# Linear attention and two MoE layers: low halves on VectorE, and the keys' maxima as a bias

## The chip, the cores and the metric

The kernel runs on one core of a Trainium2 chip. The metric is the device time of one execution in microseconds. Three executions of the kernel before and one profiled execution are at hand. The engines are called TensorE (PE in the rows, PEld for its weight loads), VectorE (DVE), ScalarE (ACT), GpSimd (POOL) and SyncE (SP), which issues most DMAs.

## What is computed

Linear attention over 8 batches, 8 heads, 576 tokens and 64 dimensions comes first, then a dense gated layer, then a layer with 8 experts of which each token takes one. The attention's features are two exponentials of a projection, from which the token's largest absolute value is taken away:

```python
def phi(x):
    proj = np.einsum('bhsd,df->bhsf', x, w_phi)
    proj = proj - np.max(np.abs(proj), axis=-1, keepdims=True)
    return np.concatenate([np.exp(proj), np.exp(-proj)], axis=-1)
q_p, k_p = phi(q), phi(k)
kv = np.einsum('bhsf,bhsd->bhfd', k_p, v)
z = np.sum(k_p, axis=2)
num = np.einsum('bhsf,bhfd->bhsd', q_p, kv)
den = np.einsum('bhsf,bhf->bhs', q_p, z)[..., None] + 1e-06
x = num / den                      # to tokens x 512
h = ((x @ w1) * (x @ w2)) @ w3
x = h @ w_out
# then: argmax of x @ w_gate, softmax weight, relu(x @ w1[e]) @ w2[e]
```

## The kernel before, in words

Every product on TensorE is made in float16 with operands cut into a high half and a low half: the high half is the value rounded to float16, the low half what is left of it, and three matmuls (high by high, high by low, low by high) make one product. So each operand that is computed on the chip needs one instruction for its high half and one subtraction for its low half.

**Attention** is done for two batches at a time (four units) and, in a unit, two heads at a time (`group`, 16 calls). A group has three steps of three token tiles (`c`) for each head `h`, 96 of them in all. For the keys: `proj` (line 543) multiplies into a PSUM tile `pj`, `k_max` (563) takes the absolute maximum `mk` of each token on VectorE, `k_sub` (569) takes it away from `pj` into an SBUF tile `pm`, `k_exp` (575) makes on ScalarE the exponential of minus `pm` (`ke2`) and, through `exp16`, the exponential of `pm` twice, once rounded to float16 into the tile `k1` and once in float32 into `e1`; `exp_lo` (559) takes one from the other on GpSimd into the low half of `k1`. `k_c1` and `k_c2` scale `ke2` into the two halves of `k2`, and `k_b` multiplies both with the values into `kv`. For the queries: `proj` and `q_max` find the maxima, `q_pj` projects again, transposed, into `pjT`, `q_exp` makes the four activations of two signs with the bias `nM`, `exp_lo` their two low halves `q1` and `q2`, `q_nm` multiplies them with the cut sums `kvs` into `nm`, `q_add` (lines 711 and 712) adds the parts into `nx`, and `q_x` (lines 719 to 723) divides into `xn`.

**The first MoE layer** (`moe1`, 12 calls of three token tiles): `ab` multiplies into two PSUM tiles `pab`, `a_out` copies one of them on ScalarE (`asb`), `g_mul` (817) multiplies on VectorE into `gf`, `g_hi` (821) rounds on ScalarE into `gt`, `g_lo` (824) makes the low half on GpSimd, and `y` (843) multiplies `gt` with the joined weights.

Beside these run the setting up of the weights (`conv64`, `moe_weight`, `w34_setup`) and the cutting of the experts' weights (`expert_weight`: line 321 on ScalarE, line 325 on VectorE, written out to DRAM). When all tokens are routed, `phase_b` runs the experts' slots.

**What sets the order.** Each step is put in a list with a time in units of its own (`at`, table `O`) and the list is written out by those times; the tile framework's scheduler then sets the order of the instructions on each engine. Every engine takes its instructions strictly in its order. Tiles share buffers by tag: `pj`, `pjT` and the experts' sums have three PSUM buffers with the tag `pj`; `nm`, `pv`, `pk`, `pq`, `pe`, `pr` and `pn` share a single one with the tag `ts`; `e1` has three buffers for keys and queries together, `q1` and `q2` two each.

Of the kernel before, what the change touches and what calls it, by code (L numbers as in the profile page):

```python
# [8 lines left out]
F32 = mybir.dt.float32  # L9
F16 = mybir.dt.float16  # L10
# [3 lines left out]
AF = mybir.ActivationFunctionType  # L14
ALU = mybir.AluOpType
# [4 lines left out]
P = 128  # L20
# [31 lines left out]
ES = 1.0 / (QS * WS)  # L52
# [12 lines left out]
def kernel(  # L65
# [16 lines left out]
    V, A, G, T = nc.vector, nc.scalar, nc.gpsimd, nc.tensor  # L82
# [23 lines left out]
    const = ctx.enter_context(tc.tile_pool(name="const", bufs=1))  # L106
    psum = ctx.enter_context(tc.tile_pool(name="psum", bufs=1, space=PSUM))
    stat = ctx.enter_context(tc.tile_pool(name="stat", bufs=2))
# [16 lines left out]
    W_B = const.tile([P, FD], F16, name="W_B")  # L125
    it8 = const.tile([P, NE], F32, name="it8")
    tri8 = const.tile([P, NE, NE], F32, name="tri8")

    def setup_a():
        nc.sync.dma_start(wphi_f[0:64, :], w_phi)  # L130
        nc.sync.dma_start(wphi_f[64:128, :], w_phi)
        V.tensor_scalar(W_A, wphi_f, WS, None, op0=ALU.mult)
        V.scalar_tensor_tensor(W_B, wphi_f, WS, W_A, op0=ALU.mult, op1=ALU.subtract)
        V.memset(zero, 0.0)

    def setup_b():
        make_identity(nc, ident32)
        V.memset(ones16, 1.0)
        V.memset(onesb, 1.0)
        V.memset(ones32, 1.0)  # L140

    def setup_c():
        G.affine_select(
            out=utri, in_=ones16, pattern=[[1, P]], compare_op=ALU.is_gt,
            fill=0.0, base=0, channel_multiplier=-1,
        )
        G.iota(rev8, pattern=[[0, 3], [-1, NE]], base=NE, channel_multiplier=0,
               allow_small_or_imprecise_dtypes=True)
        for b in range(B):
            c0 = 9 * (b // 2) + 5 * (b % 2)  # L150
            p0 = 64 * (b % 2)
            G.iota(ids[:, c0:c0 + 4], pattern=[[1, 4]], base=b * S, channel_multiplier=4)
            G.iota(ids[p0:p0 + 64, 9 * (b // 2) + 4:9 * (b // 2) + 5], pattern=[[0, 1]], base=b * S + 512,
                   channel_multiplier=1)
        G.iota(cumE, pattern=[[RG, NE]], base=0, channel_multiplier=0,
               allow_small_or_imprecise_dtypes=True)
        G.iota(it8, pattern=[[1, NE]], base=0, channel_multiplier=0, allow_small_or_imprecise_dtypes=True)
        V.memset(tri8, 1.0)
        G.affine_select(out=tri8, in_=tri8, pattern=[[1, NE], [-1, NE]], compare_op=ALU.is_ge,
                        fill=0.0, base=0, channel_multiplier=0)  # L160
# [308 lines left out]
    def group(ui, g, T0):  # L469

        bs = units[ui]
        att = pools["att"]
        h0 = 2 * g
        st = {}
# [76 lines left out]
        def exp16(key, src, sgn, nm, bufs, bias=0.0):  # L551

            hl = att.tile([P, 2, 3, P], F16, tag=nm, bufs=bufs, name=nm)
            A.activation(hl[:, 0], src, AF.Exp, scale=sgn * ES, bias=bias)  # L554
            e1 = att.tile([P, 3, P], F32, tag="e1", bufs=3, name="e1")
            A.activation(e1, src, AF.Exp, scale=sgn * ES, bias=bias)  # L556
            st[key] = (hl, e1)

        def exp_lo(key):
            hl, e1 = st[key]  # L560
            G.tensor_tensor(hl[:, 1], e1, hl[:, 0], op=ALU.subtract)  # L561

        def k_max(h, c):
            if c == 0:
# [2 lines left out]
                            apply_absolute_value=True)  # L567

        def k_sub(h, c):
            pm = att.tile([P, 3, P], F32, tag="pm", bufs=2, name="pm")  # L570
            mk = st["mk", h][:, 3 * c:3 * c + 3]
            V.tensor_tensor(pm, st["pj", "kf", h, c], mk.unsqueeze(2).to_broadcast([P, 3, P]), op=ALU.subtract)
            st["pm", h, c] = pm

        def k_exp(h, c):
            pm = st["pm", h, c]
            e2 = att.tile([P, 3, P], F32, tag="ke2", bufs=3, name="ke2")
            A.activation(e2, pm, AF.Exp, scale=-ES)
            exp16(("k1", h, c), pm, 1.0, "k1", 3)
            st["ke2", h, c] = e2  # L580

        def k_s1(h):
# [87 lines left out]

        def q_exp(c, h):
            for z in range(2):
                exp16(("q", c, h, z), st["pjT"], 1.0 - 2.0 * z, "q%d" % (z + 1), 2, st["nM"][:, 3 * h + c:3 * h + c + 1])

        def q_e1():

# [50 lines left out]
        for h in range(2):  # L727
            tv = T0 + 3 * h
            for fn in (v_load, v_norm, v_sum, v_scale, v_hi, v_lo, k_s1, k_s2, k_s3, kv_hi, kv_lo):
                at(tv + O[fn.__name__], fn, h)  # L730
            for c in range(3):
                tk = T0 + 3 * h + c
                at(tk + O["k_proj"], proj, "kf", h, c)
                for fn in (k_max, k_sub, k_exp, k_c1, k_c2, k_b):
                    at(tk + O[fn.__name__], fn, h, c)
                at(tk + O["k_lo"], exp_lo, ("k1", h, c))
        for c in range(3):
            tq = T0 + c
            at(tq + O["k_split"], split, "kf", c)
            at(tq + O["k_trans"], trans, "kf", c)  # L740
            at(T0 + O["q_sc"] * c + O["q_split"], split, "qf", c)
            at(T0 + O["q_sc"] * c + O["q_trans"], trans, "qf", c)
            for h in range(2):
                at(T0 + O["q_proj"] + O["q_pc"] * c + O["q_proj_h"] * h, proj, "qf", h, c)
                at(T0 + O["q_max"] + O["q_pc"] * c + O["q_proj_h"] * h, q_max, c, h)
                th = tq + O["q_h"] * h
                for z in range(2):
                    at(th + O["q_lo"] + O["q_lo_z"] * z, exp_lo, ("q", c, h, z))
                for fn in (q_pj, q_exp, q_nm, q_add):
                    at(th + O[fn.__name__], fn, c, h)  # L750
            at(tq + O["q_x"], q_x, c)
# [41 lines left out]
    def moe1(p, c, tk, s):  # L793
# [3 lines left out]
        st = {}  # L797
        gT = []
# [22 lines left out]
            A.copy(gT[m][:, 0, :], st["gf", m])  # L821

        def g_lo(m):
            G.tensor_tensor(gT[m][:, 1, :], st["gf", m], gT[m][:, 0, :], op=ALU.subtract)  # L824

        cw = 256 if last else 260

# [118 lines left out]
        for m in range(8):  # L946
            t = tk + m * s
            at(t, ab, m, 0)
            at(t + 0.5 * s, ab, m, 1)
            for fn in (a_out, g_mul, g_hi, g_lo):  # L950
                at(t + O[fn.__name__], fn, m)
        for n in range(3):
            t = tk + (8 + n) * s + O["y"]
# [36 lines left out]
    at(t_su * O["su_end"], su_close)  # L990
    at(0, setup_a)
    at(0.1, setup_b)
    at(1, setup_c)
    at(2, setup_d)
# [235 lines left out]
```

## Time and profile before

| | us |
|---|---|
| three executions | 1669.16, 1670.81, 1676.45 (median 1670.81) |
| the profiled execution | 1671.89 |
| its span, first to last instruction | 1670.1 |
| busy in the span: TensorE | 1429.4 (86%) |
| VectorE | 971.0 (58%) |
| ScalarE | 885.9 (53%) |
| GpSimd | 587.5 (35%) |

The shares are means over parts that differ. Attention and the first MoE layer overlap until about 1050 us; the last part of that layer and the last expert weights follow until about 1210 us; from there on the experts' slots run, with TensorE nearly always busy. The span's chain of waits breaks off in the last microseconds at the output's DMAs and tells nothing of the first part. The times of a timeline row are start and duration; an engine's next instruction often starts before the one ahead has ended, so that the distance of two starts is what an instruction takes of the engine.

### The profile page before, as it was taken

How to read it: one execution, taken by the hardware profiler on the slowest of the kernel's cores; microseconds unless marked ns; L12 is line 12 of the kernel's file. 1: busy time of each engine (PE TensorE's matmuls, PEld its weight loads, DVE VectorE, ACT ScalarE, POOL GpSimd, SP SyncE). 2: the span in 40 equal slices, each digit the busy share in tenths (PEclk: the TensorE clock that was granted, in tenths of full speed). 3: DMA queues.
4: the chain of work that ended last, by engine and by line, in shares of the span. 5: the costliest groups of instructions: out<-in, count | busy, mean ns of one | idle time of the engine just before them, and what ended most of it. 6: DMA issues, size and time to landing. Idle time of an engine off the chain costs nothing. (4 is left out here: it accounts for less than half of the span.)

```text
span 1670.1 us, 38442 instructions
## 1 busy us (share of the span) xinstructions
PE 1429.4 (86%) x14854; PEld 1029.5 (62%) x14854; DVE 971.0 (58%) x2647; ACT 885.9 (53%) x1979; POOL 587.5 (35%) x875
## 2 busy tenths in 40 slices
PE   5888868889897688977787989978949999999998
PEld 4655545656565465756465757646647777777776
DVE  6999989968878687777786886532421111111111
ACT  4787798766776567767576777433311111111111
POOL 3546553444543425434344354211312111121110
PEclk9998978989999799989988999979979999999999
DMA  6756255554257653493955464974347345646361
GB/s 198 217 143 170 64 142 124 144 150 146 71 152 124 127 157 92 119 157 89 161 157 89 139 121 112 140 248 102 70 145 188 83 77 174 221 130 173 76 172 31
DMA packets 273044, 225.17 MB, mean 135 GB/s; under 512 B 187221, under 2 KB 244825, under 8 KB 271706
## 3 DMA queue, kind: packets, MB, share of 16 engines
q1 hardware_dynamic: 265306, 202.71, 50.8%
q0 software_dynamic: 7552, 19.97, 4.1%
q8 instruction: 118, 1.93, 0.5%
q14 instruction: 68, 0.56, 0.1%
HBM read 261.22 MB, written 53.67 MB: 189 GB/s over the span
## 5 line engine op out<-in xcount | busy, mean ns | idle before, releaser
L806 PE MATMUL pab<-xT,w 128*128 128x384 f16 x768 | 263.5, 343 | 8.7 <-DVE gf L817 5.6
L1132 DVE SCALAR_TENSOR_TENSOR hT<-ph,hT 128x512 f16<-128x512 f32 x80 | 55.3, 691 | 362.0 <-ACT hT L1131 362.0
L807 PE MATMUL pab<-xT,w 128*128 128x384 f16 x768 | 262.8, 342 | 0.0
L808 PE MATMUL pab<-xT,w 128*128 128x384 f16 x768 | 262.6, 342 | 0.0
L1127 PE MATMUL ph<-xTb,wb 128*128 128x128 f16 x1280 | 218.1, 220 | 22.5 <-DMA xTb<-rw 22.5
L1128 PE MATMUL ph<-xTb,wb 128*128 128x128 f16 x1280 | 218.1, 220 | 0.0
L1129 PE MATMUL ph<-xTb,wb 128*128 128x128 f16 x1280 | 218.1, 220 | 0.0
L843 PE MATMUL py<-w,gt 128*128 128x260 f16 (+1 forms) x1728 | 205.5, 275 | 12.4 <-ACT yb L850 9.2
L561 POOL TENSOR_TENSOR q<-e,q 128x384 f16<-128x384 f32 x192 | 188.7, 992 | 65.1 <-ACT e L556 60.8
L843 PEld LDWEIGHTS <-gt 128*128 128x128 f16 x1728 | 166.3, 99 | 36.4 <-issue 9.3
L824 POOL TENSOR_TENSOR gt<-gf,gt 128x384 f16<-128x384 f32 x96 | 96.2, 1003 | 182.0 <-ACT gt L821 176.6
L561 POOL TENSOR_TENSOR k<-e,k 128x384 f16<-128x384 f32 x96 | 96.4, 1004 | 159.3 <-ACT k L554 89.3
L702 PE MATMUL nm<-kvs,q 128*128 128x65 f16 (+1 forms) x1920 | 90.1, 204 | 70.2 <-DVE nx L712 35.9
L1131 ACT ACTIVATE hT<-ph 128x512 f16<-128x512 f32 x80 | 47.8, 597 | 187.1 <-PE ph L1129 187.1
L1127 PEld LDWEIGHTS <-wb 128*128 128x128 f16 x1280 | 125.8, 98 | 27.7 <-DMA xTb<-rw 21.2
L702 PEld LDWEIGHTS <-q 128*128 128x128 f16 (+1 forms) x1920 | 79.0, 107 | 100.1 <-issue 47.3
L325 DVE SCALAR_TENSOR_TENSOR pc<-wf,ess,pc 128x512 f16<-128x512 f32 x128 | 104.6, 834 | 47.2 <-ACT pc L321 47.0
L1128 PEld LDWEIGHTS <-wb 128*128 128x128 f16 x1280 | 125.8, 98 | 4.5
L554 ACT ACTIVATE q<-pjT,nM 128x384 f16<-128x384 f32 x192 | 114.4, 596 | 26.0 <-PE nm L702 19.6
L1129 PEld LDWEIGHTS <-wb 128*128 128x128 f16 x1280 | 125.8, 98 | 0.0
L1150 ACT ACTIVATE ob<-pob,scb 128x512 f32<-128x512 f32 x40 | 27.5, 688 | 183.4 <-PE pob L1148 183.4
L626 PE MATMUL kv<-vs,k 128*128 128x65 f16 x1920 | 90.6, 198 | 37.5 <-ACT k L604 23.3
(255 smaller groups left out, 3483.6 us busy)
## 6 DMA issues: line engine op xcount, KB each, us to landing
wb<-wscr SPq DMA_DIRECT2D x40, 4096.0 KB
wf<-in_moe_w_dram SPq DMA_DIRECT2D x16, 2048.0 KB
wscr<-pc SPq DMA_DIRECT2D x128, 256.0 KB
raw<-in_moe_w_dram SPq DMA_DIRECT2D x32, 512.0 KB
rows_d<-row SPq DMA_DIRECT2D x32, 256.5 KB
kf<-in_k_dram SPq DMA_DIRECT2D x64, 128.0 KB
vf<-in_v_dram SPq DMA_DIRECT2D x64, 128.0 KB
qf<-in_q_dram SPq DMA_DIRECT2D x64, 128.0 KB
```

The costliest lines, as they stand in the source:

```text
L325: V.scalar_tensor_tensor(pc[:, 1, :], st["wf"][:, j * 512:(j + 1) * 512], st["s"][:, 0:1], pc[:, 0, :], op0=ALU.mult, op1=ALU.subtract)
L554: A.activation(hl[:, 0], src, AF.Exp, scale=sgn * ES, bias=bias)
L561: G.tensor_tensor(hl[:, 1], e1, hl[:, 0], op=ALU.subtract)
L702: T.matmul(nm[p0:p1, t, z, :], lhsT=hl[:, a, t, p0:p1], rhs=st["kvs"][:, b, h, z, bb, :], start=(a == b), stop=bool(a), skip_group_check=True)
L806: T.matmul(ps, lhsT=wh, rhs=xT[:, 0, kk], start=(kk == 0), stop=False)
L807: T.matmul(ps, lhsT=wh, rhs=xT[:, 1, kk], start=False, stop=False)
L808: T.matmul(ps, lhsT=wl, rhs=xT[:, 0, kk], start=False, stop=(kk == 3))
L824: G.tensor_tensor(gT[m][:, 1, :], st["gf", m], gT[m][:, 0, :], op=ALU.subtract)
L843: T.matmul(py, lhsT=gT[i][:, a, t * P:(t + 1) * P], rhs=w34[:, i, b, hf, 0:cw], start=(i == 0 and a == b), stop=bool(i == 7 and a))
L1127: T.matmul(ph[:, mm, :], lhsT=wh, rhs=xT[:, 0, kk, :], start=(kk == 0), stop=False)
L1128: T.matmul(ph[:, mm, :], lhsT=wh, rhs=xT[:, 1, kk, :], start=False, stop=False)
L1129: T.matmul(ph[:, mm, :], lhsT=wl, rhs=xT[:, 0, kk, :], start=False, stop=(kk == 3))
```

## The change

Three things are changed. `exp_lo` and `g_lo` are given to VectorE (`V` for `G`). `k_sub` no longer makes the tile `pm`; it makes six numbers per partition, the three maxima times -ES and times ES (`kb`, by the constants `sgn`), and `k_exp` reads `pj` in PSUM and takes these as the bias of the activation. As a bias is one number per partition and each of the three token tiles has its own, the three activations of 384 columns become nine of 128. The buffers of `q1` and `q2` are three instead of two.

```diff
+        V.memset(sgn[:, 0:1], -ES)
+        V.memset(sgn[:, 1:2], ES)
...
         def exp_lo(key):
             hl, e1 = st[key]
-            G.tensor_tensor(hl[:, 1], e1, hl[:, 0], op=ALU.subtract)
+            V.tensor_tensor(hl[:, 1], e1, hl[:, 0], op=ALU.subtract)
...
         def k_sub(h, c):
-            pm = att.tile([P, 3, P], F32, tag="pm", bufs=2, name="pm")
+            kb = stat.tile([P, 2, 3], F32, tag="kb", bufs=2, name="kb")
             mk = st["mk", h][:, 3 * c:3 * c + 3]
-            V.tensor_tensor(pm, st["pj", "kf", h, c], mk.unsqueeze(2).to_broadcast([P, 3, P]), op=ALU.subtract)
-            st["pm", h, c] = pm
+            V.tensor_tensor(kb, mk.unsqueeze(1).to_broadcast([P, 2, 3]), sgn.unsqueeze(2).to_broadcast([P, 2, 3]), op=ALU.mult)
+            st["kb", h, c] = kb
 
         def k_exp(h, c):
-            pm = st["pm", h, c]
+            pj, kb = st["pj", "kf", h, c], st["kb", h, c]
+            hl = att.tile([P, 2, 3, P], F16, tag="k1", bufs=3, name="k1")
+            e1 = att.tile([P, 3, P], F32, tag="e1", bufs=3, name="e1")
             e2 = att.tile([P, 3, P], F32, tag="ke2", bufs=3, name="ke2")
-            A.activation(e2, pm, AF.Exp, scale=-ES)
-            exp16(("k1", h, c), pm, 1.0, "k1", 3)
+            for dst, z in ((hl[:, 0], 0), (e1, 0), (e2, 1)):
+                for t in range(3):
+                    A.activation(dst[:, t, :], pj[:, t, :], AF.Exp, scale=-ES if z else ES, bias=kb[:, z, t:t + 1])
+            st["k1", h, c] = (hl, e1)
...
-                exp16(("q", c, h, z), st["pjT"], 1.0 - 2.0 * z, "q%d" % (z + 1), 2, st["nM"][:, 3 * h + c:3 * h + c + 1])
+                exp16(("q", c, h, z), st["pjT"], 1.0 - 2.0 * z, "q%d" % (z + 1), 3, st["nM"][:, 3 * h + c:3 * h + c + 1])
...
         def g_lo(m):
-            G.tensor_tensor(gT[m][:, 1, :], st["gf", m], gT[m][:, 0, :], op=ALU.subtract)
+            V.tensor_tensor(gT[m][:, 1, :], st["gf", m], gT[m][:, 0, :], op=ALU.subtract)
```

The scheduler sets the orders anew. On VectorE, in the seventh group, these rows lead from a query's second sum `nx` to the second `xn`, before:

```order
L711 TENSOR_TENSOR nx<-nm,wq 128x195
L712 TENSOR_TENSOR nx<-nx,nm 128x195
L719 TENSOR_TENSOR rec<-nx,epq 128x6
L720 RECIPROCAL rec<-rec 128x6
L721 TENSOR_TENSOR rec<-rec,svi 128x6
L723 TENSOR_TENSOR xn<-nx,rec 128x2x3x64
```

Behind the last of them stood the splits of the next group's keys. In the changed kernel the lines from `k_sub` on are higher by 3 to 8 (564 is `exp_lo`, 719 and 720 are `nx`, 727 to 731 lead to `xn`, 825 is `gf`), and the same piece reads:

```order
L719 TENSOR_TENSOR nx<-nm,wq 128x195
L494 TENSOR_SCALAR sp<-kf 128x6x64
L720 TENSOR_TENSOR nx<-nx,nm 128x195
L825 TENSOR_TENSOR gf<-pab,asb 128x384
L727 TENSOR_TENSOR rec<-nx,epq 128x6
L564 TENSOR_TENSOR k_7391<-e_7392,k_7391 128x384
L728 RECIPROCAL rec<-rec 128x6
L569 TENSOR_REDUCE mk<-pj 128x3
L729 TENSOR_TENSOR rec<-rec,svi 128x6
L564 TENSOR_TENSOR q_7403<-e_7405,q_7403 128x384
L731 TENSOR_TENSOR xn<-nx,rec 128x2x3x64
L564 TENSOR_TENSOR q_7407<-e_7409,q_7407 128x384
```

A low half of the keys and one of the queries now stand between the reciprocal's steps, and a second of the queries right behind `xn`.

On ScalarE, in the same group, the exponentials of a keys' step (`ke`, `k` and `e`) stood beside those of the queries like this, before:

```order
L898 ACTIVATE du<-du 128x24
L578 ACTIVATE ke_6925<-pm 128x384
L554 ACTIVATE k_6927<-pm 128x384
L813 ACTIVATE asb<-pab 128x384
L556 ACTIVATE e_6929<-pm 128x384
L554 ACTIVATE q_6931<-pjT,nM 128x384
L556 ACTIVATE e_6933<-pjT,nM 128x384
```

and now (586 is the new line of `k_exp`, 557 and 559 are `exp16`):

```order
L906 ACTIVATE du<-du 128x24
L305 ACTIVATE junk,ecm<-wf 128x1024
L821 ACTIVATE asb<-pab 128x384
L586 ACTIVATE k_7180<-pj,kb 128x128 x3
L586 ACTIVATE e_7181<-pj,kb 128x128 x3
L586 ACTIVATE ke_7182<-pj,kb 128x128 x3
L557 ACTIVATE q_7192<-pjT,nM 128x384
L559 ACTIVATE e_7194<-pjT,nM 128x384
```

The nine short activations stand in one piece, `k1` and `e1` first and `ke2` last, and a copy of an MoE product that stood among the three now stands ahead of them.

## Rows read from the trace of the kernel before

**Rows 1.** Busy us of each engine (instructions), granted clock, DMA share, GB/s; first stretch.
```profile
0.00:1050.00 1050.00, 854.65 (x8941) 616.30 (x8942) 842.99 (x2283) 743.04 (x1715) 469.61 (x751) 0.93 0.57 134
```

**Rows 2.** TensorE's waits until 1060 us: us in total, times, longest us.
```profile
PE nm L702 <- DVE nx L712: 35.9, 14, 7.5
...
PE pv L521 <- DVE nx L712: 22.3, 12, 4.1
...
PE nm L702 <- POOL q L561: 7.0, 12, 1.2
...
PE pj L547 <- DVE pm L572: 5.4, 3, 3.0
```

**Rows 3.** Timeline of VectorE: start us, us, instruction.
```profile
438.80 4.60 DVE L719 TENSOR_TENSOR rec<-nx,epq 128x6 f32<-128x6 f32 x1
```

**Rows 4.** Timeline of GpSimd at the same time.
```profile
438.98 1.79 POOL L561 TENSOR_TENSOR q<-e,q 128x384 f16<-128x384 f32 x2
...
441.59 1.78 POOL L561 TENSOR_TENSOR q<-e,q 128x384 f16<-128x384 f32 x2
```

**Rows 5.** Timeline of VectorE from 216 us, with GpSimd idle.
```profile
216.07 0.35 DVE L493 SCALAR_TENSOR_TENSOR sp<-kf,sp 128x192 f16<-128x192 f32 x1
216.34 0.16 DVE L719 TENSOR_TENSOR rec<-nx,epq 128x6 f32<-128x6 f32 x1
...
217.46 0.15 DVE L721 TENSOR_TENSOR rec<-rec,svi 128x6 f32<-128x6 f32 x1
217.53 0.15 DVE L600 TENSOR_SCALAR fke<-fk 128x1 f32<-128x1 f32 x1
...
217.66 0.55 DVE L723 TENSOR_TENSOR xn<-nx,rec 128x384 f32<-128x384 f32 x1
218.13 0.14 DVE L194 TENSOR_SCALAR vss<-vsh 128x1 int32<-128x1 int32 x1
```

**Rows 6.** VectorE's groups by line: busy us, mean ns | idle us before, releasers.
```profile
L572 DVE TENSOR_TENSOR pm<-pj,mk 128x384 f32<-128x384 f32 x96 | 52.4, 546 | 0.5 <-ACT k L554 0.4
...
L493 DVE SCALAR_TENSOR_TENSOR sp<-qf,sp 128x192 f16<-128x192 f32 x96 | 49.4, 528 | 0.5
...
L493 DVE SCALAR_TENSOR_TENSOR sp<-kf,sp 128x192 f16<-128x192 f32 x96 | 42.9, 471 | 0.4
...
L723 DVE TENSOR_TENSOR xn<-nx,rec 128x384 f32<-128x384 f32 x48 | 35.4, 737 | 0.6
...
L719 DVE TENSOR_TENSOR rec<-nx,epq 128x6 f32<-128x6 f32 x48 | 28.9, 601 | 0.8
...
L721 DVE TENSOR_TENSOR rec<-rec,svi 128x6 f32<-128x6 f32 x48 | 16.6, 346 | 0.6
```

**Rows 7.** GpSimd's groups by line, same columns.
```profile
L561 POOL TENSOR_TENSOR q<-e,q 128x384 f16<-128x384 f32 x192 | 188.7, 992 | 65.1 <-ACT e L556 60.8 <-issue 1.8
...
L824 POOL TENSOR_TENSOR gt<-gf,gt 128x384 f16<-128x384 f32 x96 | 96.2, 1003 | 182.0 <-ACT gt L821 176.6 <-issue 5.1
L561 POOL TENSOR_TENSOR k<-e,k 128x384 f16<-128x384 f32 x96 | 96.4, 1004 | 159.3 <-ACT k L554 89.3 <-ACT e L556 69.3
```

**Rows 8.** Two pieces of ScalarE's timeline.
```profile
402.43 0.51 ACT L554 ACTIVATE k<-pm 128x384 f16<-128x384 f32 x1
402.85 0.43 ACT L633 ACTIVATE kvs<-kv 128x130 f16<-128x130 f32 x2
403.17 0.51 ACT L821 CAST gt<-gf 128x384 f16<-128x384 f32 x1
...
420.47 0.57 ACT L556 ACTIVATE e<-pjT,nM 128x384 f32<-128x384 f32 x1
420.93 0.58 ACT L554 ACTIVATE q<-pjT,nM 128x384 f16<-128x384 f32 x1
```

**Rows 9.** ScalarE's waits until 1060 us.
```profile
ACT ke L578 <- DVE pm L572: 25.9, 25, 3.8
ACT q L554 <- PE nm L702: 19.6, 18, 2.2
```

More of the change, by code (lines that the diff above doesn't have):

```diff
@@ L127 @@
     tri8 = const.tile([P, NE, NE], F32, name="tri8")
+    sgn = const.tile([P, 2], F32, name="sgn")
     def setup_a():
```

## The prediction

> **What bounds the kernel now.** I read the busy time by stages first, then who waited for whom on TensorE and ScalarE, then the groups that the change touches, and last two short timelines of VectorE and one of ScalarE. In the first 1050 us the reader is to see four engines side by side [rows 1]: TensorE 855 us busy (81%), VectorE 843 (80%), ScalarE 743 (71%), GpSimd 470 (45%). No engine is full, so the stage is held by TensorE and VectorE waiting for each other: TensorE is idle for 195 us there, and the two largest of its waits that concern us end with VectorE's `nx` at line 712, 35.9 us before the `nm` matmuls and 22.3 us before `pv` [rows 2]. Both take the one PSUM buffer with the tag `ts`, which `nx` gives back. GpSimd is hardly waited for: 7.0 us in 12 waits before `nm` [rows 2]. The change touches the first stage, and in the 160 us after it only the 96 gated products' tail; the experts' loop runs no touched line.
>
> A second thing to see is how GpSimd and VectorE get in each other's way. At 438.8 us `rec` at line 719, six elements per partition, takes 4.60 us [rows 3], and it ends at 443.4, together with the run of five GpSimd subtractions that began at 438.98 [rows 4] (rows of two and two are shown, a fifth lies between them). At 216.34, with no GpSimd row beside it, the same instruction takes 0.16 us [rows 5]. So the mean of 601 ns [rows 6] is mostly waiting inside the instruction, and VectorE's 843 us hold time that is no work.
>
> **The low halves.** 288 subtractions at line 561 and 96 at line 824 leave GpSimd, where they take 992, 1004 and 1003 ns [rows 7], together 381 us of its 470 (a few of line 824's lie after 1050). On VectorE no such subtraction is in the trace. The nearest row is `xn` at line 723, also 384 elements out of two tensors in SBUF: 0.55 us alone, and the next instruction starts 0.47 us after it [rows 5]. I count starts, since neighbours overlap: 384 x 0.47 = +180 us. The upper end is the same group's mean beside GpSimd, 737 ns [rows 6], 283 us; I take 0.47, since the neighbours that stretch it are what moves.
>
> **The keys' maxima.** 96 subtractions `pm` of 546 ns [rows 6], less the same 0.08 us of overlap, leave VectorE: 96 x 0.47 = -45 us. In their place come 96 products of six elements; of such small instructions the next starts 0.07 us after (217.46 to 217.53) [rows 5], so +7 us. Together with the low halves VectorE gets +142 us of work.
>
> **What the lock gives back.** With the moved subtractions gone, instructions that wait inside get short. Group by group, mean less the time alone [rows 5, 6]: line 719, 48 x (0.601 - 0.16) = 21 us; line 721, 48 x (0.346 - 0.15) = 9; line 723, 48 x (0.737 - 0.55) = 9; the splits at line 493, 96 x (0.528 - 0.35) = 17 for the queries and 96 x (0.471 - 0.35) = 12 for the keys. That is 68 us in five groups. Other groups that read SBUF twice I leave uncounted; as an estimate they give at most as much again, 136. I take 100. So VectorE's busy time would go from 843 to about 885 us (84%), between 849 and 917.
>
> The Trainium skill (GPSIMD Engine Reference, Specifications) says that GpSimd shares its SBUF interfaces with VectorE, with contention where a VectorE instruction has two SBUF inputs or runs in a 2-port mode. The trace agrees as far as rows go: line 719 reads two SBUF tensors and stretches from 0.16 to 4.60 us. It speaks a little against the change too, since `pm` read PSUM once and the low halves read SBUF twice, and so become exposed to what GpSimd keeps; by this the 180 us would move toward 283, and the sum by up to +50.
>
> **ScalarE.** `k_exp` was three activations of 384 columns out of SBUF, starting 0.42 us apart (402.43 to 402.85) [rows 8]: 1.26 us. Now it is nine of 128 columns out of PSUM, each with a bias per partition. The nearest in size are the two of 130 columns at 402.85, out of PSUM without a bias: both within 0.32 us, 0.16 each [rows 8]. A bias out of a tile costs something: 384 columns out of PSUM with one start 0.46 us apart (420.47 to 420.93), against 0.42 out of SBUF without [rows 8]. I take 0.25, nine are 2.25 us, +1.0 us x 96 = +96 us, which puts ScalarE at 839 us (80%) in the stage. The ends: 9 x 0.16 = 1.44 us, +17 us in all; and 9 x 0.29, if these do not overlap as the 0.43 us for two suggest they may not, 2.6 us, +130.
>
> The Trainium skill (ScalarE: Activation LUTs, What ACT_TABLE_LOAD costs) gives 280 ns + 0.833 ns per column for an activation with such a bias and 93 ns of overlap. An estimate from it is 0.29 us for 128 columns, 9 x 0.29 = 2.6 us and +131 us on ScalarE; the sum below would be 5 us longer. No row here has this form.
>
> **Buffers.** The query exponentials get a third buffer. ScalarE waited 19.6 us for `nm` before them [rows 9]; I count half of this as gained on the path, -10, with ends 0 and -20. The key projections' PSUM buffer (tag `pj`, three for both projections) was free after `pm`, 0.47 us after the maximum; now the last of nine activations frees it, at least 0.07 + 2.25 us after the maximum, and later where ScalarE has a queue. Each of 96 holds lasts about 1.85 us longer. Today TensorE waits 5.4 us for `pm` there [rows 2], and 25 of ScalarE's 96 exponentials start right after `pm` (25.9 us) [rows 9], so in about three of four ScalarE comes later than `pm`. I count +5 us, with ends 0 and 96 x 1.85 = 178.
>
> **Order.** The scheduler has put low halves between VectorE instructions that TensorE waits for: between the two `nx` and the `xn` shown ahead there are now two, and one more behind. The low half also waits for ScalarE's second exponential, and behind it in VectorE's queue stand `nx` and the maxima; on GpSimd nothing that TensorE needs stood behind such a wait.
>
> **How much lies on the path.** VectorE is busy 80% of the stage and TensorE 81%; an added microsecond on VectorE lies on the path at most in 0.8, at least where it falls into VectorE's idle fifth, in none. For the added work I choose 0.5, because the low halves of the gated product come while TensorE has its long MoE matmuls. For what the lock gives back I choose 0.6, since lines 719 to 723 stand directly behind the `nx` that TensorE waits for. ScalarE's extra time I count at 0.15: it is the least loaded of the three.
>
> **The sum**, on the profiled execution's 1671.9 us (the median of the three is 1670.8, so 1 us apart): +142 x 0.5 = +71; -100 x 0.6 = -60; the hop over GpSimd that TensorE waited for, -7 [rows 2]; third buffer -10; ScalarE 96 x 0.15 = +14; PSUM buffer +5. Together +13, so 1685 us, 0.8% slower.
>
> **The rivals.**
> *The lock decides: faster.* The five stretched groups are on the way from `nm` to `xn`, and the low halves fall into VectorE's gaps. Then 136 x 0.7 = -95, 142 x 0.4 = +57, -7, -10, ScalarE +14: -41, 1631 us. For it: a single 4.60 us stall in front of `xn`. Against it: VectorE has only 207 us of gaps.
> *The terms cancel.* With a share of 0.6 for the lock and 0.42 for the added work the sum is 0: 1672 us.
> *The PSUM buffer decides: clearly slower.* If ScalarE, now at 80%, frees `pj` late in one of three holds, 178 / 3 = +59 comes on top of the forecast's other terms: 1685 - 5 + 59 = 1739. It decides from the point where TensorE reaches the third next projection before the ninth activation ends. For it: both engines that hold `pj` are now busy four fifths. Against it: 5.4 us of such waits today.
> *The change doesn't free VectorE.* If the low halves wait on VectorE for what GpSimd keeps (470 - 381 = 89 us) or for ScalarE's results, and no lock time comes back, the forecast loses its -60: 1745.
>
> **How the numbers follow.** Half a percent, 8 us, is about what a measurement of this kernel can tell from no change. Forecast (slower by 0.5 to 3%) 0.38, its own range 1680 to 1720; the lock decides 0.32; cancel 0.14; the PSUM buffer 0.10; no lock time back 0.06. So faster 0.32, same 0.14, slower 0.54. The range has to reach both sides: 1622 leaves out about a tenth, the lower part of the lock case (its terms allow -50), and 1745 less than a tenth, the upper parts of the last two.
>
> **What would show it.** Lines 719 and 721 (727 and 729 in the changed kernel) at 0.15 to 0.2 us mean confirm the lock; if they stay over 0.4 that step is wrong. The low halves on VectorE near 0.55 us long, VectorE between 849 and 917 us in the first stage, the nine activations 0.25 us apart. TensorE's waits for `nx` at 36 us or more speak for the forecast, far under it for the lock; waits of the projections for the key exponentials of tens of us for the PSUM buffer. Wrong altogether would be the forecast if VectorE's work in the stage falls under 843.

## The result and the profile after

Four runs of the changed kernel took 1652.95 us in the median (1647.39 to 1661.13), four of the kernel before 1673.63 us (1669.16 to 1677.64): a ratio of 0.9885, with a 95% interval of 0.986 to 0.991. It is faster by 1.2%, where 0.8% slower was forecast. The runs below were made on other occasions, on which the kernel before took 1650 to 1653 us; so kernels of different occasions are compared by their ratio to the kernel before that ran beside them. The changed kernel's own ratio was 0.989 on the first occasion and 0.981 to 0.983 on three later ones, so between occasions a difference under about 0.7% shows nothing.

The first stretch after, of the profiled execution of 1661.1 us (busy us of TensorE, its weight loads, VectorE, ScalarE, GpSimd with their instructions, then granted clock, DMA share, GB/s):

```profile
0.00:1050.00 1050.00, 871.51 (x9031) 625.55 (x9036) 852.24 (x2694) 843.52 (x2315) 130.03 (x396) 0.92 0.61 136
```

Against [rows 1], GpSimd fell from 470 to 130 us, ScalarE rose from 743 to 844 (839 was forecast), and VectorE, which took over 384 subtractions, rose by 9 us only. What it gained back is to be seen in its groups (busy us, mean ns, then idle time before):

```profile
L564 DVE TENSOR_TENSOR q<-e,q 128x384 f16<-128x384 f32 x192 | 105.7, 555 | 11.0 <-ACT e L559 10.3
...
L564 DVE TENSOR_TENSOR k<-e,k 128x384 f16<-128x384 f32 x96 | 54.0, 563 | 27.5 <-ACT e L586 27.2
...
L832 DVE TENSOR_TENSOR gt<-gf,gt 128x384 f16<-128x384 f32 x96 | 53.0, 552 | 21.7 <-ACT gt L829 21.5
...
L496 DVE SCALAR_TENSOR_TENSOR sp<-kf,sp 128x192 f16<-128x192 f32 x96 | 34.2, 373 | 0.2
...
L496 DVE SCALAR_TENSOR_TENSOR sp<-qf,sp 128x192 f16<-128x192 f32 x96 | 32.1, 351 | 0.3
...
L731 DVE TENSOR_TENSOR xn<-nx,rec 128x384 f32<-128x384 f32 x48 | 27.0, 563 | 0.2
...
L575 DVE TENSOR_TENSOR kb<-mk,sgn 128x6 f32<-128x6 f32 x96 | 15.5, 162 | 0.2 <-ACT ke L586 0.2
...
L729 DVE TENSOR_TENSOR rec<-rec,svi 128x6 f32<-128x6 f32 x48 | 8.1, 170 | 0.2
L727 DVE TENSOR_TENSOR rec<-nx,epq 128x6 f32<-128x6 f32 x48 | 7.6, 159 | 0.3
```

The low halves take 0.55 to 0.56 us, and the groups of [rows 6] have come down to what they take alone: the two steps of `rec` from 601 and 346 ns to 159 and 170, the splits from 528 and 471 to 351 and 373, `xn` from 737 to 563. Over all of VectorE's groups, taking what lies above each group's lower quartile (where it is 60 ns and more), the time spent waiting inside instructions was 139 us before and is 10 us now. Of the 139 us, 132 lay in instructions that ran beside GpSimd's subtractions.

TensorE's waits until 1060 us (total, times, longest):

```profile
PE nm L710 <- DVE nx L720: 39.2, 15, 12.0
PE pj L550 <- ACT ke L586: 28.8, 13, 10.8
PE pv L524 <- DVE nx L720: 17.6, 5, 14.6
...
PE nm L710 <- DVE q L564: 4.5, 5, 1.9
```

The waits for `nx` are much as in [rows 2], and there is a new one: the projections wait 28.8 us for a `pj` buffer that the keys' last exponential holds. On ScalarE the nine activations of a step come three by three:

```profile
406.56 0.88 ACT L586 ACTIVATE k<-pj,kb 128x128 f16<-128x128 f32 x3 [0.17 <-PE kv L634]
407.33 0.89 ACT L586 ACTIVATE e<-pj,kb 128x128 f32<-128x128 f32 x3
408.08 0.92 ACT L586 ACTIVATE ke<-pj,kb 128x128 f32<-128x128 f32 x3
408.83 0.51 ACT L641 ACTIVATE kvs<-kv 128x130 f16<-128x130 f32 x2
```

From 407.33 to 408.83 six of them take 1.50 us: 0.25 each, as the forecast took it.

### The profile page after: what moved, and what is told of

It reads as the page before. It is cut to its first block, busy times and chain, and to the rows that moved or that the text cites. A ratio compares the mean times of both kernels' runs of the same rounds, so it can differ in the third digit from the quotient of the medians.

```text
span 1659.4 us, 38809 instructions
## 1 busy us (share of the span) xinstructions
PE 1434.0 (86%) x14850; PEld 1032.1 (62%) x14854; DVE 978.4 (59%) x3033; ACT 975.2 (59%) x2555; POOL 221.3 (13%) x491
## 5 line engine op out<-in xcount | busy, mean ns | idle before, releaser
L851 PE MATMUL py<-w,gt 128*128 128x260 f16 (+1 forms) x1728 | 212.5, 277 | 11.1 <-ACT yb L858 7.8
L324 ACT ACTIVATE pc<-wf,ess 128x512 f16<-128x512 f32 x128 | 94.9, 766 | 61.4 <-DMA wscr<-pc 46.1
L557 ACT ACTIVATE q<-pjT,nM 128x384 f16<-128x384 f32 x192 | 125.7, 655 | 6.9 <-PE pjT L676 6.7
L559 ACT ACTIVATE e<-pjT,nM 128x384 f32<-128x384 f32 x192 | 126.4, 660 | 1.3 <-DVE q L564 1.2
L1154 PE MATMUL pob<-wb,hT 128*128 128x512 f16 x320 | 121.3, 379 | 0.0
L1155 PE MATMUL pob<-wb,hT 128*128 128x512 f16 x320 | 121.3, 379 | 0.0
L1156 PE MATMUL pob<-wb,hT 128*128 128x512 f16 x320 | 121.3, 379 | 0.0
```

Of the source, the lines that this page charges most:

```text
L851: T.matmul(py, lhsT=gT[i][:, a, t * P:(t + 1) * P], rhs=w34[:, i, b, hf, 0:cw], start=(i == 0 and a == b), stop=bool(i == 7 and a))
L1154: T.matmul(po, lhsT=hT[:, 0, i2, :], rhs=wh, start=(i2 == 0), stop=False)
L1155: T.matmul(po, lhsT=hT[:, 0, i2, :], rhs=wl, start=False, stop=False)
```

## The experiments

My theory after the result: the gain is the lock, that is, VectorE's instructions no longer wait inside for GpSimd. The rivals: the bias, the third query buffer, or the shorter way of the low halves.

**The parts one at a time.** `lo_alone` moves the low halves only:

```diff
-            G.tensor_tensor(hl[:, 1], e1, hl[:, 0], op=ALU.subtract)
+            V.tensor_tensor(hl[:, 1], e1, hl[:, 0], op=ALU.subtract)
...
-            G.tensor_tensor(gT[m][:, 1, :], st["gf", m], gT[m][:, 0, :], op=ALU.subtract)
+            V.tensor_tensor(gT[m][:, 1, :], st["gf", m], gT[m][:, 0, :], op=ALU.subtract)
```

> The kernel before, with the 384 low halves on VectorE and nothing else changed (the keys' subtraction pm stays, two buffers for the query exponentials). The lock theory (the gain comes from VectorE no longer waiting inside its instructions for GpSimd): the reciprocal lines 719 and 721 at about 0.16 us mean, VectorE 843 + 180 - 130 = about 893 us busy in the first 1050 us, ScalarE at 743, and most of the gain is there: 1650 to 1662 us. The rival (taking pm off VectorE is what pays, the low halves alone overload it): 1675 to 1700 us.

Measured: 1632.5 us, ratio 0.988 (0.985 to 0.990). The expected microseconds were set for the first occasion's 1674 us and are read through the ratio, here as below: 1650 to 1662 us are 0.986 to 0.993. VectorE's groups and first stretch:

```profile
L719 DVE TENSOR_TENSOR rec<-nx,epq 128x6 f32<-128x6 f32 x48 | 7.5, 157 | 0.0
...
0.00:1050.00 1050.00, 895.12 (x9223) 645.99 (x9228) 885.83 (x2717) 759.35 (x1756) 131.50 (x397) 0.93 0.62 143
```

The low halves alone give as much as the whole change gave on the first occasion, with VectorE 43 us busier in the first 1050 us than before. Every edit also gives the scheduler new orders to make, here on all engines; what that does by itself is taken up below.

`bias_alone` has the changed `k_sub` and `k_exp`, and nothing else:

> The kernel before, with the maxima as a bias and the low halves left on GpSimd, two query buffers. The lock theory: the waits inside VectorE's instructions stay (lines 719 and 721 over 0.35 us mean), VectorE gets 38 us less and ScalarE 100 us more, the projections wait some 30 us for their PSUM buffer: no gain, 1670 to 1700 us. The rival (the bias is what pays): 1650 to 1660 us.

Measured: 1679.7 us, ratio 1.017 (1.014 to 1.020). The bias alone costs 1.7%, 28 us, slightly more than the slowest that was expected (1700 us, a ratio of 1.016).

`two_buffers` is the changed kernel with one edit undone:

```diff
-                exp16(("q", c, h, z), st["pjT"], 1.0 - 2.0 * z, "q%d" % (z + 1), 3, ...
+                exp16(("q", c, h, z), st["pjT"], 1.0 - 2.0 * z, "q%d" % (z + 1), 2, ...
```

> The changed kernel with two buffers for the query exponentials again, as before. The lock theory gives the third buffer little: 1653 to 1663 us. The rival, that ScalarE's freedom to run ahead of the matmuls (19.6 us of waits before, none after) carries the gain: 1668 to 1678 us.

Measured: 1637.8 us, ratio 0.991 (0.989 to 0.994), 5 to 6 us slower than `lo_alone` with intervals that overlap. It told nothing of the third buffer yet, since the changed kernel had run on another occasion.

**The lock by itself.** `pool_repeats` is `two_buffers` with GpSimd's traffic put back, into a tile that nobody reads:

```diff
             V.tensor_tensor(hl[:, 1], e1, hl[:, 0], op=ALU.subtract)
+            jk = att.tile([P, 3, P], F16, tag="jk", bufs=1, name="jk")
+            G.tensor_tensor(jk, hl[:, 0], hl[:, 0], op=ALU.subtract)
```

and the same behind `g_lo`.

> The kernel of two_buffers, in which GpSimd makes 384 subtractions besides, each out of the float16 high half into a tile that nobody reads, at the places where the low halves are made on VectorE. Nothing waits for them, so the way of the data is as in two_buffers, only GpSimd's traffic is back. The lock theory: VectorE's instructions wait inside again (reciprocal lines back over 0.35 us, VectorE over 950 us busy in the first 1050 us, the low halves on VectorE over 0.65 us), and the time is 30 to 100 us over two_buffers. The rival, that the shorter way over VectorE in place of GpSimd is the gain: within 8 us of two_buffers.

Measured: 1733.0 us, ratio 1.048 (1.046 to 1.051), 5.7% or 94 us over `two_buffers`. The low halves on VectorE got longer too, and `rec` is stretched again:

```profile
L564 DVE TENSOR_TENSOR q<-e,q 128x384 f16<-128x384 f32 x192 | 139.7, 731 | 6.6 <-ACT e L559 5.8
...
L729 DVE TENSOR_TENSOR rec<-nx,epq 128x6 f32<-128x6 f32 x48 | 16.6, 345 | 0.1
...
L731 DVE TENSOR_TENSOR rec<-rec,svi 128x6 f32<-128x6 f32 x48 | 13.0, 270 | 0.3
...
0.00:1050.00 1050.00, 823.90 (x8290) 582.32 (x8295) 917.40 (x2489) 789.59 (x2158) 438.73 (x717) 0.90 0.55 129
```

TensorE, VectorE and ScalarE run their instructions in the same order in the two traces, and of their waits in `pool_repeats` until 1300 us only 1.8 us on ScalarE and 4.7 us on VectorE (4.9 in `two_buffers`) end with GpSimd. So work of GpSimd whose results nobody needs costs 94 us by what it does to VectorE. VectorE's waiting inside instructions, counted as above, rose from 10 to 158 us; 94 / 148 is a share of 0.64. The two `rec` came to 0.35 and 0.27 us, where over 0.35 was expected, and the first stretch shows 917 us where over 950 were, since less of the work falls into it.

**The changed kernel beside its neighbours.** `after_again`, `nine_from_pm`, `exp_lo_only` and `lo_twice` ran together.

> The changed kernel itself, on the chip of the runs beside it. Ratio to before 0.986 to 0.991, as first measured. Theory (the low halves carry the gain, the bias takes a little of it back, the third buffer gives nothing): slower than lo_alone by 3 to 8 us and within 5 us of two_buffers' ratio of 0.991. Rival (the third buffer pays): a ratio under 0.986.

Measured: 1621.9 us, ratio 0.983 (0.979 to 0.986). That is better than on the first occasion and spoke for the rival.

`nine_from_pm` is `lo_alone` with the nine activations on ScalarE, but without the longer hold of PSUM:

```diff
-            A.activation(e2, pm, AF.Exp, scale=-ES)
-            exp16(("k1", h, c), pm, 1.0, "k1", 3)
+            hl = att.tile([P, 2, 3, P], F16, tag="k1", bufs=3, name="k1")
+            e1 = att.tile([P, 3, P], F32, tag="e1", bufs=3, name="e1")
+            for dst, z in ((hl[:, 0], 0), (e1, 0), (e2, 1)):
+                for t in range(3):
+                    A.activation(dst[:, t, :], pm[:, t, :], AF.Exp, scale=-ES if z else ES, bias=zb[:, 0:1])
```

> lo_alone, in which the keys' exponentials are nine activations of 128 columns out of pm in SBUF, with a tensor of zeros as their bias. ScalarE gets the same work as in the changed kernel or a little more (+100 us in the first stage), but pm stays, so PSUM is free as early as in lo_alone and VectorE keeps its 45 us. If ScalarE's time is what the bias costs: 6 to 25 us over lo_alone. If it is the PSUM buffer that is held longer: within 5 us of lo_alone.

Measured: 1631.1 us, ratio 0.988 (0.985 to 0.992), as `lo_alone`. ScalarE has 117 us more in the first stretch than in `lo_alone`, and the time is the same:

```profile
0.00:1050.00 1050.00, 893.75 (x9181) 639.31 (x9186) 890.50 (x2712) 876.38 (x2329) 127.40 (x396) 0.93 0.63 140
...
PE pj L550 <- DVE pm L575: 7.3, 9, 1.8
```

So nothing here shows ScalarE's time as the price of the bias, with the reserve that the orders of `lo_alone` and `nine_from_pm` differ. The bias takes `pm` off VectorE (1001 to 981 us busy in the whole run from `lo_alone` to `two_buffers`) and is still 5 to 12 us slower; a row that differs is the projections' wait for their PSUM buffer, here 7.3 us, with the bias 18.5 us in `two_buffers`:

```profile
PE pj L550 <- ACT ke L586: 18.5, 14, 4.3
```

With the low halves on GpSimd that row is short (5.5 us in `bias_alone`), so for the 28 us which the bias costs there it is no full answer.

`exp_lo_only` is `lo_alone` with `g_lo` on GpSimd.

> lo_alone with the gated product's 96 low halves back on GpSimd. The lock theory: VectorE's excess from waits comes back by some 25 us (the share that overlapped line 824 before), VectorE loses 45 us of work, so the time is 0 to 10 us over lo_alone. The rival (in the MoE stretch VectorE's work was better left on GpSimd): 5 to 15 us under lo_alone.

Measured: 1627.5 us, ratio 0.986 (0.982 to 0.989), the same as `lo_alone` within the intervals. VectorE's waiting inside is 36 us instead of 9, as expected; against that stand 45 us less of work on VectorE.

`lo_twice` makes each subtraction of `lo_alone` twice:

```diff
             V.tensor_tensor(hl[:, 1], e1, hl[:, 0], op=ALU.subtract)
+            V.tensor_tensor(hl[:, 1], e1, hl[:, 0], op=ALU.subtract)
```

> lo_alone with each of the 384 subtractions made twice on VectorE, the second over the first. VectorE gets 384 x 0.47 = 180 us more in the first stage and the early tail, GpSimd nothing. This measures the disputed share of added VectorE work that lies on the path: at 0.5, as forecast, +90 us over lo_alone; at 0.35, as the sum after the result would have it, +63 us; if VectorE's gaps take most of it, under +40 us.

Measured: 1767.4 us, ratio 1.071 (1.067 to 1.075), 8.3% or 137 us over `lo_alone`. For 180 us of work that is a share of 0.76, more than any of the theories had. The scheduler's order is another one here too.

**The third buffer.** The changed kernel, `lo_alone` and `two_buffers` ran once more, side by side, with `after_g_pool`, the changed kernel with `g_lo` on GpSimd.

> The changed kernel again, beside lo_alone and two_buffers on one chip. Its two ratios so far are 0.9885 and 0.9827 on two occasions, so it is to be compared with its neighbours here. If the bias costs and the third buffer gives nothing: 3 to 8 us over lo_alone and as two_buffers. If the third buffer pays for the bias: 5 to 12 us under two_buffers and within 5 us of lo_alone.

> The changed kernel with two query buffers, again: ratio 0.989 to 0.994 as before. Its distance to the changed kernel is what the third buffer is worth: 0 by my theory, 5 to 12 us by the rival.

> The low halves alone, again: ratio 0.985 to 0.990 as before. If bias and third buffer together pay, it is slower than the changed kernel by over 5 us; if they don't, faster or the same.

> The changed kernel with the 96 low halves of the gated product on GpSimd again, which lo_alone stood as well without as with. If those 96 are neutral: within 5 us of the changed kernel. If VectorE's load is the bound by now (the 180 us more of lo_twice cost over 130 us): 5 to 20 us under it. If the lock they bring back (27 us inside VectorE's instructions in exp_lo_only) counts more: 5 to 15 us over it.

Measured: the changed kernel 1622.4 us, 0.982 (0.979 to 0.985); `two_buffers` 1640.7 us, 0.994 (0.992 to 0.996); `lo_alone` 1630.0 us, 0.987 (0.983 to 0.991); `after_g_pool` 1644.7 us, 0.995 (0.993 to 0.997). My theory of the third buffer fell: beside the bias and the low halves on VectorE it is worth 18 us, with the new order that it brings (VectorE's differs in some 430 places). And here the 96 low halves of the gated product do count, 22 us, where they were neutral in `lo_alone`. One row that changes with the third buffer is ScalarE's wait in front of the query exponentials, 10.2 us in `two_buffers`, which is gone in the changed kernel:

```profile
ACT q L557 <- PE nm L710: 10.2, 7, 5.2
```

Another is TensorE's wait for the scaled keys before `kv`, in `two_buffers` and then in the changed kernel, while its wait for `pj` went the other way (18.5 and 28.8 us):

```profile
PE kv L634 <- ACT k L612: 16.7, 14, 7.0
```
```profile
PE kv L634 <- ACT k L612: 7.5, 9, 2.5
```

These rows don't add up to 18 us; by which way the rest comes is open.

Is it the buffer itself, or does it only make up for the bias? `lo_three` and `pool_three` get the room for it by writing `pm` into the tile of `ke2`, without a bias:

```diff
-            pm = att.tile([P, 3, P], F32, tag="pm", bufs=2, name="pm")
+            pm = att.tile([P, 3, P], F32, tag="ke2", bufs=3, name="ke2")
...
-            e2 = att.tile([P, 3, P], F32, tag="ke2", bufs=3, name="ke2")
-            A.activation(e2, pm, AF.Exp, scale=-ES)
             exp16(("k1", h, c), pm, 1.0, "k1", 3)
-            st["ke2", h, c] = e2
+            A.activation(pm, pm, AF.Exp, scale=-ES)
+            st["ke2", h, c] = pm
```

> The changed kernel, beside the three others on one chip: ratio 0.980 to 0.989.

> lo_alone with a third buffer for the query exponentials, and no bias. The room for it comes from writing pm into the tile of ke2, where the exponential of minus pm then overwrites it. If the buffer pays by itself: 10 to 18 us under lo_alone's ratio of 0.987, so 0.976 to 0.981, and faster than the changed kernel. If it only makes up for the bias: 0.984 to 0.990.

> The kernel before, low halves on GpSimd and no bias, with the third query buffer, by the same sharing of pm and ke2. If the buffer pays by itself: 8 to 18 us under before. If it only pays where the low halves are on VectorE or the bias is there: within 5 us of before.

> The changed kernel with the low halves on GpSimd: bias and third buffer alone. bias_alone was 1.017. If the buffer pays whatever the low halves do: 1.004 to 1.010. If its gain needs the low halves on VectorE: 1.013 to 1.020.

Measured: the changed kernel 1623.6 us, 0.981 (0.979 to 0.983); `lo_three` 1624.8 us, 0.983 (0.981 to 0.985); `pool_three` 1651.4 us, 1.000 (0.998 to 1.002); `bias_three` 1684.2 us, 1.018 (1.016 to 1.021). All together, as ratios to the kernel before:

| | low halves on GpSimd | low halves on VectorE |
|---|---|---|
| `pm`, two buffers | 1 | 0.988, 0.987 |
| `pm`, three buffers | 1.000 | 0.983 |
| bias, two buffers | 1.017 | 0.991, 0.994 |
| bias, three buffers | 1.018 | 0.989, 0.983, 0.982, 0.981 |

Bias and third buffer bring nothing, or a loss, while GpSimd makes the low halves. With these on VectorE the buffer gives about 1% beside the bias. Without the bias it seems to give 0.4%, between the two branches of what was expected; the intervals of `lo_three` and `lo_alone` overlap, and they ran on different occasions, so that is not shown. `lo_three` shows that the bias isn't needed: it is as fast as the changed kernel.

**The terms of the low halves apart.** What 148 us of lock cost in `pool_repeats` (94 us) and what 180 us of work cost in `lo_twice` (137 us) would make the low halves on VectorE a loss, and they are a gain. So one of two more terms had to be far off: the hop over GpSimd (what TensorE loses by waiting for a low half that GpSimd makes), or the share of the first 180 us. `low_unread` is the kernel before, with TensorE reading the high half where it read these low halves, so that their correction is left out of the sums, and `no_low` the same without GpSimd's subtractions:

```diff
-                            T.matmul(nm[p0:p1, t, z, :], lhsT=hl[:, a, t, p0:p1],
+                            T.matmul(nm[p0:p1, t, z, :], lhsT=hl[:, 0, t, p0:p1],
```

and in the same way for `k1` and `gt`.

> The kernel before, in which TensorE reads the high half again in place of the 384 low halves that GpSimd makes: the correction by these low halves is left out of the sums. GpSimd and VectorE do all that they did, TensorE does the same number of matmuls, but nothing on TensorE waits for GpSimd. If the hop over GpSimd was worth 50 us and more: a ratio under 0.972. If it was worth the 7 us that TensorE waited for it: 0.990 to 1.000.

> The same without GpSimd's 384 subtractions: the low halves are neither made nor read. Against low_unread only the lock goes (some 130 us inside VectorE's instructions): 80 us less at the share of 0.63 that pool_repeats gave. Against lo_alone (0.987) it shows what the first 180 us of VectorE work cost: 60 us or less (no_low at 0.950 or over) if the first lie on the path less than the second, 130 us (about 0.91) if they lie on it as the second did.

Measured: `low_unread` 1658.0 us, ratio 1.004 (1.002 to 1.006); `no_low` 1572.0 us, 0.951 (0.949 to 0.953). `rec` and the first stretch of the one, then of the other:

```profile
L719 DVE TENSOR_TENSOR rec<-nx,epq 128x6 f32<-128x6 f32 x48 | 27.7, 578 | 0.8
...
0.00:1050.00 1050.00, 861.11 (x8973) 622.63 (x8974) 850.29 (x2304) 746.67 (x1725) 471.43 (x751) 0.93 0.55 135
```
```profile
L719 DVE TENSOR_TENSOR rec<-nx,epq 128x6 f32<-128x6 f32 x48 | 7.7, 160 | 0.8
...
0.00:1050.00 1050.00, 903.08 (x9452) 658.18 (x9453) 755.52 (x2405) 776.57 (x1798) 122.50 (x402) 0.95 0.63 152
```

The hop over GpSimd costs nothing: without it the kernel is, if anything, slower. The lock costs 1.004 - 0.951, 5.3% or 87 us, a share of 0.65 of the 134 us by which the waiting inside falls (141 to 7). And the first 180 us of low halves on VectorE cost 0.987 - 0.951, 3.6% or 60 us: a share of 0.33, against 0.76 for the second.

How clean are these two? In `low_unread` and `no_low` TensorE, VectorE and ScalarE have the same order of instructions, and until 1300 us of `low_unread` no matmul waits for GpSimd and VectorE does for 9 us in all. TensorE's waits that end with VectorE are what falls, from 148 to 89 us. Nothing but GpSimd's subtractions is gone, so the 87 us are the lock. The whole run of `low_unread` (span 1660.4 us), `no_low` (1573.7) and `lo_alone` (1625.2):

```profile
PE 1431.4 (86%) x14854; PEld 1033.7 (62%) x14854; DVE 974.1 (59%) x2647; ACT 886.3 (53%) x1979; POOL 589.7 (36%) x875
```
```profile
PE 1397.8 (89%) x14854; PEld 1020.6 (65%) x14854; DVE 844.2 (54%) x2647; ACT 879.6 (56%) x1979; POOL 209.5 (13%) x491
```
```profile
PE 1429.0 (88%) x14850; PEld 1031.8 (63%) x14854; DVE 1001.2 (62%) x3031; ACT 882.6 (54%) x1979; POOL 222.3 (14%) x491
```

With the lock gone VectorE's same instructions take 130 us less, TensorE is idle 53 us less, and its matmuls take 34 us less at a granted clock of 0.95 instead of 0.93 in the first stretch. The 60 us are not as clean: from `no_low` to `lo_alone`, as from there to `lo_twice`, the scheduler has made other orders (VectorE's differ in some 500 places each time), so both shares hold what the order does. And of the 51 us between the profiled executions of `no_low` and `lo_alone`, TensorE's idle time is only 20; the other 31 are matmuls that took longer, the clock being 0.93 again.

## Why the prediction was wrong

**The sum of the low halves is where it failed.** Forecast were +90 us for the work (180 x 0.5), -60 for the lock and -7 for the hop, +23 in all. Measured they are +60, -87 and about +6, which is -21 us, the 1.2 to 1.3% of `lo_alone` against before. (They are the steps from one kernel to the next on the way from before to `lo_alone`, so that they add up is no proof of each; the lock has its own in `pool_repeats`.)

*The share of the added work* was the larger miss, 30 us. I took 0.5 starting from VectorE's 80% of busy time [rows 1], although I had just read that these 843 us hold time that is no work: some 126 of them were waits that the change itself removes (136 in the stretch before, 10 after). Without such waits VectorE is busy 756 us of the stretch in `no_low` (72%, and the stretch holds more of the program by then), and the first 180 us cost a third of their length, with the new order and the clock in it. The share is no constant: the next 180 us, on an engine at 886 us, cost 0.76. The step that read "VectorE has only 207 us of gaps" was wrong in the same way, since by this count the room was about 333.

*The size of the lock* was mis-sized by 27 us. I counted 68 us in five groups and took 100; it was 129 to 134. The doubling that I named as the upper end, 136, was the value. The share of 0.6 was about right (0.64 and 0.65).

*The hop* was a small term, and it was none: GpSimd's 7.0 us of waits in [rows 2] are gone in `low_unread`, and the time did not fall.

**The rest of the sum.** The duration of the low halves (0.47 us from start to start, 0.55 long), of the nine activations (0.25 us, +96 us on ScalarE; the measured +101) and of the small product (162 ns long, 0.07 taken) held. VectorE's 852 us lay inside 849 to 917, at its low end. ScalarE's share of 0.15 was too high: 117 us more cost nothing in `nine_from_pm`. The estimate of 0.29 us from one start to the next, worked out from the Trainium skill's figures (ScalarE: Activation LUTs, What ACT_TABLE_LOAD costs), gave way to the measured 0.25 for this form out of PSUM; out of SBUF, in `nine_from_pm`, the trace has 0.29. The stretching of the low halves by what GpSimd keeps, for which up to 50 us were allowed, did not come: their means are 552 to 563 ns. VectorE's 38 us less were credited with -19; with ScalarE and PSUM the bias came to 0, and it cost 28 us alone and 5 to 12 us beside the low halves. Of the PSUM buffer's rival the mechanism was there (28.8 us of waits where 5.4 had been), its price far under the 59 us named. The third buffer's -10 was -18 beside bias and low halves and 0 without them; a buffer's worth can't be added up on its own. What the prediction feared of the order, low halves between the instructions that TensorE waits for, was not timed apart from the rest; the two waits for `nx` were 58 us before and 57 after.

**The rival that came true** was the lock, whose price I put at 1631 us by a share of 0.7 for 136 us and 0.4 for the added work. Those two were close to the measured 0.65 and 0.33. Its sign was the one that I said would show it: the two `rec` at 0.16 and 0.17 us. The condition that I read against it, too few gaps, was the mistaken one. And "TensorE's waits for `nx` at 36 us or more" did not speak for the forecast: they stayed at 39 us while the time fell.

What stays open is why the bias costs 28 us while the low halves are on GpSimd, and how the third buffer gains 18 us beside bias and low halves. The new orders are a candidate for both, and no run holds them still.

## What to carry to other kernels

Before an engine's busy time is used as its load, look for groups whose mean lies far over what the same instruction takes alone; a six-element instruction of 0.6 us is a wait, and it belongs to the other engine's work. When work is moved onto an engine, estimate its share on the path with that engine's load as it will be after the move, and expect the second portion to cost more than the first (here 0.33, then 0.76). A bundle of edits is best timed apart and in pairs: here one edit made the gain, one cost time, and a third paid only where the first was in. And where a scheduler orders the instructions, look whether two kernels run them in the same order before a difference is put down to the edit: here it held for the two pairs that show the lock, and for hardly another.

## What the runs showed of the hardware

An instruction of VectorE that reads two SBUF tensors can wait inside for a whole run of GpSimd's: 4.60 us for six elements [rows 3, 4]. Such long ones are few, seven of over 1 us in the kernel before; most of the 139 us are shorter waits. `pm`, which reads a large operand from PSUM, took 546 ns beside GpSimd's subtractions [rows 6] and 548 without them in `no_low`. Two SBUF operands are not needed for it: the rounding of the keys, `sp` from the one tensor `kf`, took 488 ns in `low_unread` and 373 in `no_low`. 381 us of such work on GpSimd cost the kernel 87 us without any result of it being used (`low_unread` against `no_low`). The low halves of the queries, 555 ns alone and 731 ns beside GpSimd's repeats in `pool_repeats`, are exposed in the same way.

With more work on VectorE TensorE was granted less of its clock: the mean of the first stretch was 0.95 in `no_low`, 0.93 in `lo_alone` and 0.88 in `lo_twice`, and TensorE was busy 903, 895 and 825 us of it. The same program's matmuls took 1398, 1429 and 1478 us in all, so part of what a load on VectorE costs is paid in longer matmuls. The stretch in `lo_twice`:

```profile
0.00:1050.00 1050.00, 825.25 (x8109) 586.34 (x8114) 937.36 (x2734) 683.36 (x1568) 123.08 (x379) 0.88 0.54 124
```
